# Row maxima of attention as a two-part row: the split moved to columns, the transpose to a product

## The chip, the cores and the metric

The kernel runs on one core of a Trainium2 chip. The core has a matrix engine (TensorE; in the profile PE for its products and PEld for the loading of weights), three elementwise engines (VectorE or DVE, ScalarE or ACT, GpSimd or POOL) and a queue that issues transfers (SyncE or SP). The metric is the device time of one execution in microseconds (us): 1706.35 us for the kernel before, the median of three runs from 1704.84 to 1709.86.

## The reference

One block of a transformer with adaptive layer norm, 2048 tokens of 512 features in fp32:

```python
mod = (_silu(c) @ w_mod).reshape(c.shape[0], 6, 1, -1)
sa, ca, ga, sb, cb, gb = (mod[:, 0], ..., mod[:, 5])
h = _layernorm(x, axis=-1) * (1 + ca) + sa
x = x + ga * attention(h, A_wqkv, A_wo)      # 32 heads of 16, full softmax
h = _layernorm(x, axis=-1) * (1 + cb) + sb
x = x + gb * (mish(h @ B_w1 + B_b1) @ B_w2)  # 512 -> 1792 -> 512
```

The change lies in the softmax of the attention, `softmax(q k^T / 4)`: for each head and each query the maximum over the 2048 keys is taken off before the exponential.

## The kernel before

**Numbers in two parts.** Most products run in float32r, a rounded form of fp32. To keep the precision, a number is split in a high part (rounded to float32r) and a low part (what is left), and a product is made of three: high by high, high by low, low by high. For the attention the split lies along the contraction: a head has 16 features, which become 48 rows of an operand (`ka` for keys, `qa` for queries), two heads to a tile at partitions 0 and 64. Rows 48 to 63 of each half are extra: in `ka` they hold constants (the tile `one`, stored there once in the prologue, copied on for the later buffers), in `qa` zeros, and in rows 48 and 49 of `qa` later the negative maximum of each query in two parts. A score product then gives the score less its maximum at once, since the key's extra rows multiply it by the constants.

**Groups and steps.** Work is cut in 32 groups (`n`): 4 blocks of 512 queries by 8 sets of 4 heads. A group takes 16 steps of the main loop (`step(t)`), each of four kinds of work on TensorE:

- four maxima products (`max_tile`, L482): 128 queries by 512 keys into a slot of a ring of six PSUM banks (`ring()`), each followed by a reduction on VectorE (L484) into a column of `mx`. These belong to a later group: the maxima run 20 steps (`PRO`) ahead of the scores.
- four score products (L531), 128 keys by 512 queries, each into a slot of the same ring, followed by the exponential on ScalarE (L534), which writes `pr`.
- the product of the exponentials with the values (`pv`, L549), called PV below, for the four heads of the step before the last.
- a part of other work (L135): the projections of the first layer, later the output projection and the feed-forward layers, in halves of 64 rows that stand beside the products above.

The order of all instructions is written out by hand: `step` emits maxima and scores in turn, with the other work in between, then PV. Hooks (`at`) put transfers and elementwise work at half steps. A ring slot is taken again six products later, after the reduction or exponential that reads it.

**The rows of maxima.** At the end of the step in which the last maximum of a group is emitted, `neg_max` (L500) reduces the four partial maxima of each query to one. It writes them twice, by two reductions (L505), into `mm`: 128 queries by 32 columns, which are 4 (half and head pair) by 2 (high and low place) by 4 (part of the block). One step later `max_rows` (L509) turns `mm` into rows: a transpose on TensorE against the identity `ident` (L511) into a ring slot, the negated high part rounded to float32r by ScalarE into `mh` (L513), and on VectorE (L514) `mt = mh * lows - slot`, where `lows` is -1 in the rows of the low places and 0 in the others: the high places get the negated maximum rounded by the write, the low ones what is left. Then four transfers of 4 KB (L520) store the rows of `mt` into rows 48 and 49 of the four halves of `qa`. The scores that read them start four steps after the maxima are complete.

Of the kernel before, what the change touches and what calls it, by code (L numbers as in the profile page):

```python
# [8 lines left out]
F32 = mybir.dt.float32  # L9
F32R = mybir.dt.float32r  # L10
AF = mybir.ActivationFunctionType
ALU = mybir.AluOpType
AX = mybir.AxisListType
# [5 lines left out]
def adaln_block(ctx: ExitStack, tc: tile.TileContext, x, wqkv, wo, w1, b1, w2, c, w_mod, out):  # L19
    nc = tc.nc  # L20
    P = 128
# [25 lines left out]
    out = out[0]  # L47
# [3 lines left out]
    cst = ctx.enter_context(tc.tile_pool(name="cst", bufs=1))  # L51
# [11 lines left out]
    ident = cst.tile([P, P], F32, name="ident")  # L63
# [10 lines left out]
    nc.gpsimd.memset(sel, 0.0)  # L74
    for k in range(DK):
        nc.gpsimd.memset(sel[32 * k:32 * k + 1, :], 1.0)
    lows = cst.tile([P, 1], F32, name="lows")
    nc.vector.tensor_reduce(out=lows[:32], in_=ident[:32, :32].rearrange("p (a v q) -> p v a q", a=4, v=2)[:, 1], op=ALU.add,
                            axis=AX.XY)
    nc.vector.tensor_scalar_mul(lows[:32], lows[:32], -1.0)  # L80
    modc = cst.tile([P, 4, DK], F32, name="modc")
    sil = cst.tile([P, DK], F32, name="sil")
    b1c = cst.tile([P, FT], F32, name="b1c")
# [66 lines left out]
    def ring(w=1):  # L150
        if w == 2 and ring_at[0] % 2:
            ring_at[0] += 1
        b = ring_at[0] % NRING
        ring_at[0] += w
        return ring_t[:, b, :] if w == 1 else ring_t[:, b:b + 2, :]
# [41 lines left out]
    def at(h, f):  # L197

        hooks.setdefault(h, []).append(f)
# [121 lines left out]
    with ExitStack() as es:  # L321
# [24 lines left out]
        nc.gpsimd.memset(zer, 0.0)  # L346
        one = lp.tile([P, TB], F32, name="one")
        nc.gpsimd.memset(one, 1.0)

        e = lp.tile([P, DK], F32, name="sil_e")  # L350
        nc.scalar.activation(e, cc, AF.Exp, scale=-1.0)
# [38 lines left out]
        for i in range(2):  # L390
            pr.append(ring())
            for k in range(DK):
                nc.tensor.matmul(pr[i][32 * k:32 * k + 32, :], sil[:, k:k + 1].to_broadcast([P, 32]), wma[i][:, k, :],
                                 start=True, stop=True)
# [68 lines left out]
    ap = ctx.enter_context(tc.tile_pool(name="ap", bufs=1, reuse_waits="tile"))  # L463
# [36 lines left out]
    def neg_max(n):  # L500

        mx = mxs.pop(n)
        mm = ap.tile([P, 4, 2, 4], F32, tag="mm", name="mm", bufs=2)
        for v in range(2):
            nc.vector.tensor_reduce(out=mm[:, :, v, :], in_=mx.rearrange("p s (j q) k -> p (s j) q k", j=2), op=ALU.max,  # L505
                                    axis=AX.X)
        ats.setdefault(16 * n + 16 - PRO, []).append(lambda: max_rows(n, mm))

    def max_rows(n, mm):  # L509
        pt = ring()  # L510
        nc.tensor.transpose(pt[:32, :P], mm.rearrange("p a v q -> p (a v q)"), ident)  # L511
        mh, mt = [ap.tile([32, P], F32R, tag=t, name=t, bufs=1) for t in ("mh", "mt")]
        nc.scalar.activation(mh, pt[:32, :P], AF.Identity, scale=-1.0)  # L513
        nc.vector.scalar_tensor_tensor(mt, mh.bitcast(F32), lows[:32], pt[:32, :P], op0=ALU.mult, op1=ALU.subtract)  # L514

        def put():
            for s in (1, 0):
                for j in range(2):
                    o = (2 * s + j) * 8
                    nc.sync.dma_start(  # L520
                        qa[(2 * n + j) % NR][64 * s + 48:64 * s + 50, :].rearrange("v (s q) -> v s q", s=4).bitcast(F32),
                        mt[o:o + 8, :].bitcast(F32))
        at(2 * (16 * n + 16 - PRO) + 2, put)
# [649 lines left out]
    def step(t):  # L1173
# [4 lines left out]
        if t < 0:  # L1178

            for i in range(2):  # L1180
                if tm < 16:
                    kb, jq = divmod(2 * tm + i, 8)
                else:
                    jq, kb = tm % 16 // 2, 2 * second + i
                max_pair(tm // 16, jq, kb)
            if second and tm % 16 == 15:
                neg_max(tm // 16)
            run_hooks(2 * t + 1)
            for f in ats.pop(t, []):
                f()  # L1190
            whole_units(2 * t + 1, CREDIT)
            do_specials(2 * t + 1)
            return
# [58 lines left out]
        if tm < T and tm % 16 == 15:  # L1252
            neg_max(tm // 16)
# [111 lines left out]
    t = T + 2  # L1365
# [32 lines left out]
```

## Time and profile before

| what | value |
|---|---|
| median of three runs | 1706.35 us (1704.84 to 1709.86) |
| profiled execution, span from first to last instruction | 1705.4 us |
| mean granted TensorE clock | 0.998 of full speed |
| TensorE products busy | 1678.7 us, 98% |
| VectorE busy | 1439.9 us, 84% |
| ScalarE busy | 1364.9 us, 80% |
| GpSimd busy | 808.0 us, 47% |

The span of the profiled execution is 0.95 us below the median of the runs. A row of a timeline gives start and length in us, engine, line, operation, what is written and read, and in brackets the idle time of the engine before it with what ended that time. A group of instructions gives the count after x, busy time in us, the mean of one in ns, and the idle time before them. Products are pipelined and their ends are modelled, so a busy TensorE is not TensorE at its peak.

### The profile page before, as it was taken

What the parts mean: (1) busy time and instruction counts of PE and PEld (TensorE: products, weight loads), DVE (VectorE), ACT (ScalarE), POOL (GpSimd) and SP (SyncE); (2) the same over time, 40 slices, a digit from 0 to 9 for tenths busy, and PEclk for the clock granted to TensorE, in tenths of its full rate; (3) what the DMA queues carried; (4) which work ended last, traced back from release to release, by engine and by line L of the source; (5) the groups of instructions that cost most, each with busy time, mean ns of one, the idle gap of its engine ahead of it and who ended that gap; (6) DMA issues with size and microseconds to landing.
All of it is one profiled execution on the core that took longest, in us unless ns stands there. A gap on an engine that the chain in (4) does not pass through costs nothing.

```text
span 1705.4 us, 33628 instructions
## 1 busy us (share of the span) xinstructions
PE 1678.7 (98%) x12372; PEld 956.8 (56%) x12372; DVE 1439.9 (84%) x2368; ACT 1364.9 (80%) x2613; POOL 808.0 (47%) x829
## 2 busy tenths in 40 slices
PE   7999999999999999999999999999999999999999
PEld 5755655555445555555555555555555455554587
DVE  6888888888889998888889998888889988883377
ACT  6257777777778988888888988888888988888574
POOL 5155224665413464655423564555323655555442
PEclk9999999999999999999999999999999999999999
DMA  7677467777773342534355433424354433524261
GB/s 253 183 235 210 116 161 213 242 228 221 237 209 100 98 105 78 137 79 123 84 154 145 119 75 94 139 74 125 85 144 124 128 93 78 150 59 156 85 228 63
DMA packets 113997, 240.08 MB, mean 141 GB/s; under 512 B 24048, under 2 KB 49648, under 8 KB 107784
## 3 DMA queue, kind: packets, MB, share of 16 engines
q1 hardware_dynamic: 113832, 237.92, 48.8%
q8 instruction: 98, 1.61, 0.4%
q14 instruction: 67, 0.55, 0.1%
HBM read 179.95 MB, written 51.44 MB: 136 GB/s over the span
## 4 chain that ended last, share of the span: by engine, by line
PE 90%; DMA 4%; DVE 3%; ACT 1%; SPq 1%; issue 1%; POOL 0%; ACTq 0%; DVEq 0%; POOLq 0%
PE bk L549 28%; PE ring L482 21%; PE ring L531 19%; PE bk L135 12%; PE bk L129 3%; PE ring L1110 2%; PE ring L129 2%; DVE mx L484 1%; DMA qa<-mt 1%; DMA ka<-kscr 1%; DMA xt<-in_A_x 1%; PE ring L496 1%; ACT pr L534 1%; DMA w<-woscr 1%; DMA w<-w1scr 0%
## 5 line engine op out<-in xcount | busy, mean ns | idle before, releaser
L484 DVE TENSOR_REDUCE mx<-ring 128x1 f32<-128x512 f32 x1968 | 1222.1, 682 | 157.7 <-PE ring L482 134.1
L534 ACT ACTIVATE pr<-ring 128x512 f32<-128x512 f32 x2048 | 1085.6, 601 | 215.5 <-PE bk L135 131.2
L482 PE MATMUL ring<-ka,qa 64*128 64x512 f32 x1968 | 834.2, 427 | 5.2 <-DMA od<-ot 2.7
L531 PE MATMUL ring<-qa,ka 64*128 64x512 f32 x2048 | 724.5, 397 | 4.2 <-ACT pr L534 2.2
L482 PEld LDWEIGHTS ring<-ka,qa 64*128 64x128 f32 x1968 | 359.6, 184 | 405.8 <-DVE mx L484 341.2
L549 PE MATMUL bk<-pr,vg 128*32 128x512 f32 x4096 | 545.1, 604 | 0.0
L531 PEld LDWEIGHTS ring<-qa,ka 64*128 64x128 f32 x2048 | 373.8, 184 | 81.3 <-ACT pr L534 23.6
L135 PE MATMUL bk<-h,w 64*128 64x512 f32 (+1 forms) x1080 | 280.2, 393 | 0.1
L135 PE MATMUL bk<-w,a_h 64*128 64x512 f32 x632 | 213.0, 417 | 0.3 <-ACT pr L534 0.2
L135 PEld LDWEIGHTS bk<-h,w 64*128 64x128 f32 x1080 | 178.2, 184 | 12.3 <-ACT pr L534 3.7
L549 PEld LDWEIGHTS bk<-pr,vg 128*32 128x32 f32 x4096 | 80.7, 108 | 132.0 <-issue 124.6
L135 PE MATMUL bk<-w,a_l 64*128 64x512 f32 x316 | 124.0, 392 | 0.0
L135 PEld LDWEIGHTS bk<-w,a_h 64*128 64x128 f32 x632 | 104.7, 184 | 16.6 <-ACT pr L534 8.3
L899 POOL TENSOR_TENSOR y<-yd,y 128x512 f32<-128x512 f32 x44 | 56.8, 1292 | 89.5 <-ACT yd L898 84.4
L750 POOL TENSOR_TENSOR qq<-qq,rr 128x512 f32<-128x512 f32 x42 | 54.3, 1292 | 89.8 <-ACT rr L744 89.6
L734 POOL TENSOR_SCALAR qq<-ee 128x512 f32<-128x512 f32 x25 | 15.5, 619 | 168.0 <-ACT ee L728 168.0
L736 POOL TENSOR_TENSOR hb<-hb,ee 128x512 f32<-128x512 f32 x42 | 54.1, 1288 | 82.5 <-DVE ee L732 80.5
L135 PE MATMUL bk<-w,o_hl 64*128 64x512 f32 x288 | 79.6, 408 | 0.0
L98 POOL TENSOR_TENSOR a_l<-hb,a_h 128x512 fp32r<-128x512 f32 x53 | 72.0, 1359 | 4.4
L135 PEld LDWEIGHTS bk<-w,a_l 64*128 64x128 f32 x316 | 58.3, 184 | 3.9
L135 PE MATMUL bk<-h_h,wl 64*128 64x512 f32 x168 | 56.7, 418 | 0.0
L752 POOL TENSOR_TENSOR rr<-rr,qq 128x512 f32<-128x512 f32 x42 | 54.2, 1291 | 3.5
(189 smaller groups left out, 1844.2 us busy)
## 6 DMA issues: line engine op xcount, KB each, us to landing
ka<-kscr SPq DMA_DIRECT2D x124, 384.0 KB
w<-w2scr SPq DMA_DIRECT2D x56, 512.0 KB
w<-w1scr SPq DMA_DIRECT2D x46, 512.0 KB
vg<-vscr SPq DMA_DIRECT2D x32, 552.0 KB
qa<-qscr SPq DMA_DIRECT2D x124, 100.0 KB
kscr<-qh SPq DMA_DIRECT2D x16, 512.0 KB
qscr<-qh SPq DMA_DIRECT2D x32, 256.0 KB
hl<-in_B_w SPq DMA_DIRECT2D x28, 256.0 KB
```

The costliest lines, as they stand in the source:

```text
L98: (nc.gpsimd if eng == "p" else nc.vector).tensor_sub(lo, src, hi.bitcast(F32))
L129: nc.tensor.matmul(acc, l, r, start=start, stop=stop)
L135: i = nc.tensor.matmul(acc, l[64 * g:64 * g + 64], r[64 * g:64 * g + 64], start=start and not g, stop=bool(stop and g))
L482: nc.tensor.matmul(pm, qt[64 * s:64 * s + 64, qs * P:(qs + 1) * P], kt[64 * s:64 * s + 64, kb * TB:(kb + 1) * TB], start=True, stop=True)
L484: nc.vector.tensor_reduce(out=mxs[n][:, s, 4 * j + qs, kb:kb + 1], in_=pm, op=ALU.max, axis=AX.X)
L531: nc.tensor.matmul(p_, kt[64 * s:64 * s + 64, kc * P:(kc + 1) * P], qt[64 * s:64 * s + 64, :], start=True, stop=True)
L534: e = nc.scalar.activation(pr, p_, AF.Exp, scale=SCALE)
L549: nc.tensor.matmul(accs[n][32 * h:32 * h + 32, :], vgs[n][:, o:o + 32], pts.pop((t, h)), start=(kc == 0), stop=(kc == 15))
L736: (nc.vector if tail else nc.gpsimd).tensor_mul(hb, hb, ee)
L750: nc.gpsimd.tensor_mul(qq, qq, rr)
L752: nc.gpsimd.tensor_mul(rr, rr, qq)
L899: nc.gpsimd.tensor_add(y[i], yd, y[i])
```

## The change

The split of the maxima moves before the turn into rows. `neg_max` now makes four reductions on VectorE, each with one operand in SBUF: the negative maximum into `nh[:, 0]`; that, negated again and rounded to float32r, into the high places of `mm`; the same into `nh[:, 1]`; and the sum of the two parts of `nh`, the negative of what the rounding left, into the low places of `mm`. The second waits for the first, and the fourth for the third. `mm` becomes float32r, so the turn into rows is an ordinary product with a rounded identity `identr`, and ScalarE copies its result into `mt`. `mh`, `lows` and the VectorE instruction of `max_rows` are gone. The high part now stands with a plus sign, so the first of the key's extra rows is -1: four rows of the tile `one`, which the store spreads as one row of 2048 keys. The order of the products on TensorE, of the instructions on ScalarE and of the transfers is the same as before; on VectorE the four reductions stand where the two stood.

```diff
-    lows = cst.tile([P, 1], F32, name="lows")
-    nc.vector.tensor_reduce(out=lows[:32], in_=ident[:32, :32].rearrange("p (a v q) -> p v a q", a=4, v=2)[:, 1], op=ALU.add,
-                            axis=AX.XY)
-    nc.vector.tensor_scalar_mul(lows[:32], lows[:32], -1.0)
+    identr = cst.tile([P, P], F32R, name="identr")
+    nc.vector.tensor_copy(identr, ident)
...
         one = lp.tile([P, TB], F32, name="one")
         nc.gpsimd.memset(one, 1.0)
+        nc.gpsimd.memset(one[:4, :], -1.0)
...
-        mm = ap.tile([P, 4, 2, 4], F32, tag="mm", name="mm", bufs=2)
-        for v in range(2):
-            nc.vector.tensor_reduce(out=mm[:, :, v, :], in_=mx.rearrange("p s (j q) k -> p (s j) q k", j=2), op=ALU.max,
-                                    axis=AX.X)
+        mm = ap.tile([P, 4, 2, 4], F32R, tag="mm", name="mm", bufs=2)
+        nh = ap.tile([P, 2, 4, 4], F32, tag="nh", name="nh", bufs=1)
+        mx = mx.rearrange("p s (j q) k -> p (s j) q k", j=2)
+        nc.vector.tensor_reduce(out=nh[:, 0], in_=mx, op=ALU.max, axis=AX.X, negate=True)
+        for hi in (mm[:, :, 0, :], nh[:, 1].bitcast(F32R)):
+            nc.vector.tensor_reduce(out=hi, in_=nh[:, 0, :, :, None], op=ALU.max, axis=AX.X, negate=True)
+        with nc.allow_low_precision(reason="the low part of a split"):
+            nc.vector.tensor_reduce(out=mm[:, :, 1, :], in_=nh.rearrange("p v a q -> p a q v"), op=ALU.add, axis=AX.X)
         ats.setdefault(16 * n + 16 - PRO, []).append(lambda: max_rows(n, mm))
 
     def max_rows(n, mm):
         pt = ring()
-        nc.tensor.transpose(pt[:32, :P], mm.rearrange("p a v q -> p (a v q)"), ident)
-        mh, mt = [ap.tile([32, P], F32R, tag=t, name=t, bufs=1) for t in ("mh", "mt")]
-        nc.scalar.activation(mh, pt[:32, :P], AF.Identity, scale=-1.0)
-        nc.vector.scalar_tensor_tensor(mt, mh.bitcast(F32), lows[:32], pt[:32, :P], op0=ALU.mult, op1=ALU.subtract)
+        nc.tensor.matmul(pt[:32, :P], mm.rearrange("p a v q -> p (a v q)"), identr, start=True, stop=True)
+        mt = ap.tile([32, P], F32R, tag="mt", name="mt", bufs=1)
+        nc.scalar.copy(mt, pt[:32, :P])
```

## The prediction

> **What bounds the kernel now.** The page comes first: the busy shares and the chain of work that ended last.
>
> ```profile
> PE 1678.7 (98%) x12372; PEld 956.8 (56%) x12372; DVE 1439.9 (84%) x2368; ACT 1364.9 (80%) x2613; POOL 808.0 (47%) x829
> ...
> PE 90%; DMA 4%; DVE 3%; ACT 1%; SPq 1%; issue 1%; POOL 0%; ACTq 0%; DVEq 0%; POOLq 0%
> ```
>
> TensorE carries 90% of the chain. VectorE is busy 84% of the span but on 3% of the chain, so an edit on it counts only where it makes TensorE wait. Next, the groups by line, each shape apart, for the instructions that the change touches:
>
> ```profile
> L505 DVE TENSOR_REDUCE mm<-mx 128x16 f32<-128x64 f32 x64 | 11.1, 215 | 1.1
> ...
> L514 DVE SCALAR_TENSOR_TENSOR mt<-mh,lows,ring 32x128 fp32r<-32x128 f32 x32 | 10.7, 333 | 15.9 <-ACT mh L513 15.9
> ...
> L511 PE MATMUL ring<-ident,mm 128*32 128x128 f32 x32 | 9.1, 284 | 0.0
> L513 ACT ACTIVATE mh<-ring 32x128 fp32r<-32x128 f32 x32 | 8.5, 266 | 11.0 <-PE ring L511 11.0
> ```
>
> The touched code runs 32 times, once in 16 steps of the main loop; everything on VectorE that goes is 10.7 + 15.9 us busy and idle. How far TensorE sees that is read from the timeline of one boundary between two groups (start, length, engine, instruction, and in brackets idle time and its releaser):
>
> ```profile
> 750.59 0.16 PEld L549 LDWEIGHTS bk<-pr,vg 128*32 128x32 f32 x8 [0.24 <-issue]
> ...
> 751.58 0.18 PEld L482 LDWEIGHTS ring<-ka,qa 64*128 64x128 f32 x1 [0.84 <-DVE mx L484]
> ...
> 751.80 0.35 DVE L505 TENSOR_REDUCE mm<-mx 128x16 f32<-128x64 f32 x2
> ...
> 752.12 2.48 DVE L484 TENSOR_REDUCE mx<-ring 128x1 f32<-128x512 f32 x4
> ...
> 752.86 0.18 PEld L531 LDWEIGHTS ring<-qa,ka 64*128 64x128 f32 x1
> ...
> 753.00 0.18 PEld L482 LDWEIGHTS ring<-ka,qa 64*128 64x128 f32 x1
> ...
> 753.42 0.16 PEld L549 LDWEIGHTS bk<-pr,vg 128*32 128x32 f32 x8 [0.24 <-issue]
> ...
> 754.42 0.09 PEld L511 LDWEIGHTS ring<-ident,mm 128*32 128x32 f32 x1 [0.84 <-DVE mx L484]
> ...
> 754.63 0.18 PEld L482 LDWEIGHTS ring<-ka,qa 64*128 64x128 f32 x1
> ...
> 754.74 0.27 ACT L513 ACTIVATE mh<-ring 32x128 fp32r<-32x128 f32 x1 [0.33 <-PE ring L511]
> ...
> 755.04 0.33 DVE L514 SCALAR_TENSOR_TENSOR mt<-mh,lows,ring 32x128 fp32r<-32x128 f32 x1 [0.44 <-ACT mh L513]
> ...
> 755.31 2.46 DVE L484 TENSOR_REDUCE mx<-ring 128x1 f32<-128x512 f32 x4
> ...
> 755.53 1.52 ACT L534 ACTIVATE pr<-ring 128x512 f32<-128x512 f32 x3
> ...
> 756.03 0.18 PEld L531 LDWEIGHTS ring<-qa,ka 64*128 64x128 f32 x1 [0.17 <-DVE mx L484]
> ...
> 756.15 0.18 PEld L482 LDWEIGHTS ring<-ka,qa 64*128 64x128 f32 x1
> 756.58 0.16 PEld L549 LDWEIGHTS bk<-pr,vg 128*32 128x32 f32 x8 [0.25 <-issue]
> ```
>
> A step runs from one PV block (L549) to the next. The first step is 753.42 - 750.59 = 2.83 us, and TensorE never stops in it: 1.0 us of PV, then from S = 751.58 eight products into the six slots of the ring, the last two loaded at S + 1.28 and S + 1.42, and PV 0.42 after the last load. The two L505 sit in VectorE's pause (751.80 to 752.15), and the step's first reduction starts at S + 0.54, when its product is there: L505 is free now. The second step is 756.58 - 753.42 = 3.16, so 0.33 longer: the transpose holds TensorE 0.21 (754.42 to 754.63), and the rest, 0.12, is the last two loads at S' + 1.40 and S' + 1.52 (S' = 754.63), held by the late reduction (755.31) and by the late exp (755.53 + 0.60).
>
> **What a late first reduction costs** is in two other steps, where other VectorE work went in front:
>
> ```profile
> 1278.47 0.16 PEld L549 LDWEIGHTS bk<-pr,vg 128*32 128x32 f32 x8 [0.37 <-issue]
> ...
> 1279.12 3.05 DVE L484 TENSOR_REDUCE mx<-ring 128x1 f32<-128x512 f32 x5
> ...
> 1279.46 0.18 PEld L482 LDWEIGHTS ring<-ka,qa 64*128 64x128 f32 x1 [0.84 <-DVE ln_mv L105]
> ...
> 1281.02 0.18 PEld L531 LDWEIGHTS ring<-qa,ka 64*128 64x128 f32 x1 [0.33 <-DVE mx L484]
> ...
> 1281.45 0.16 PEld L549 LDWEIGHTS bk<-pr,vg 128*32 128x32 f32 x8 [0.24 <-issue]
> ```
>
> ```profile
> 578.47 0.16 PEld L549 LDWEIGHTS bk<-pr,vg 128*32 128x32 f32 x8 [0.24 <-issue]
> 579.27 3.07 DVE L484 TENSOR_REDUCE mx<-ring 128x1 f32<-128x512 f32 x5
> ...
> 579.46 0.18 PEld L482 LDWEIGHTS ring<-ka,qa 64*128 64x128 f32 x1 [0.84 <-DVE ee L732]
> ...
> 581.20 0.18 PEld L531 LDWEIGHTS ring<-qa,ka 64*128 64x128 f32 x1 [0.41 <-DVE mx L484]
> ...
> 581.63 0.16 PEld L549 LDWEIGHTS bk<-pr,vg 128*32 128x32 f32 x8 [0.24 <-issue]
> ```
>
> In each run of five the first two reductions belong to the step before. At 0.60 apart (0.58 in the first) the third starts at S + 0.82 and S + 1.00 and the load that waits for its slot follows 0.73 later, PV 0.43 after that. The steps are 2.98 and 3.16, 0.15 and 0.33 over 2.83. So a first reduction at S + x costs x - 0.68 us, and nothing below that.
>
> **The change, part by part.** The sum is made against the profiled span of 1705.4; the median of the runs, 1706.35, lies 0.95 above it, and I carry the difference over.
>
> (a) *Four dependent reductions for two, in the step of `neg_max`.* No four-link chain stands in the trace; the nearest rows are L505 and the pair that opens the program:
>
> ```profile
> 1.32 0.16 DVE L78 TENSOR_REDUCE lows<-ident 32x1 f32<-32x16 f32 x1 [1.32 <-POOL ident masks.py:199]
> 1.51 0.14 DVE L80 TENSOR_SCALAR lows<-lows 32x1 f32<-32x1 f32 x1
> ...
> 1313.73 0.18 PEld L482 LDWEIGHTS ring<-ka,qa 64*128 64x128 f32 x1 [0.84 <-DVE mx L484]
> ...
> 1313.89 0.35 DVE L505 TENSOR_REDUCE mm<-mx 128x16 f32<-128x64 f32 x2
> ```
>
> A reduction of 16 elements takes 0.16; a dependent instruction starts 0.03 after the end of its source; independent ones overlap by 0.07 (two L505 of 0.215 in 0.35). First 0.215 + 0.03, second 0.16 but the third starts 0.09 after it, third 0.16 + 0.03, fourth 0.18 (32 elements read), of which the next overlaps 0.07: 0.215 + 0.03 + 0.09 + 0.16 + 0.03 + 0.18 - 0.07 = 0.64 us from start to the step's first reduction. The chain starts at S + 0.16 to S + 0.22 (1313.89 and 751.80), so x is 0.80 to 0.86 instead of 0.54, and the cost 0.12 to 0.18, middle 0.15. Queued behind the two new waits are the step's four big reductions, and behind those TensorE's loads into their slots. VectorE catches up in the next step, where it no longer waits. The regular boundary is there some 27 times of 32: +4.1. Bounds: x 0.07 lower, 0.08 each, +2.2; 0.03 more for each of the three small links, 0.24 each, +6.5.
>
> The Trainium skill has a rule here that speaks against the change: "VectorE: DVE Perf Modes", section "Rules for kernel authors", says to lower the number of operations and not of semaphores, since each operation drains at its full length, chained or not. The trace differs: two independent L505 take 0.35, not 0.43. By the rule (a) would be +5.9 and the sum 1708.9 (rival D has the working).
>
> (b) *L514 and its wait go from VectorE.* The first reduction after the transpose can start at S' + 0.54 instead of S' + 0.68. That frees the load at 756.03, but the one at 756.15 waits for the exp, which the change leaves where it is: `mt` is copied by ScalarE, in the place and at the size of L513 (0.266; I take the copy as equal). Gain between 0 and the whole 0.12; I take 0.04, since the second load stands later: 30 x 0.04 = -1.2. If it is 0, ScalarE is late next. The wait for the former four stores of `mt` moves from L514 to this copy; they were issued 16 steps before and hide there, and queued behind it are this step's exps. Bound +0.03 each, +1.
>
> (c) *An ordinary product in place of the transpose.* Same weights (128x32), 128 moving columns. Nearest rows: L511 itself, 0.21 on TensorE; and the ordinary products into 256 columns, fifteen in 1.99, 0.133 each:
>
> ```profile
> 50.80 1.99 PE bk L129 x15
> ```
>
> Below, half of 0.133 is 0.07: gain 0.14 each, -4.5; above, 0.21 again: 0. I take 0.133, the nearest row of the new kind, as a product of half the columns can hardly be half as dear with its fixed part: 0.08 x 32 = -2.6.
>
> The Trainium skill, "VectorE: DVE Perf Modes", section on the TRN2 errata, gives a product max(60, 6 + columns) cycles at 2.4 GHz: 0.056 us here, an estimate, by which (c) would be -4.9 and the sum 1704.7. No run shows a product of 128 columns; at 256 the trace has 0.133 where the formula gives 0.109.
>
> (d) *Prologue.* In block 0 TensorE waits for the second L505:
>
> ```profile
> 93.47 0.09 PEld L511 LDWEIGHTS ring<-ident,mm 128*32 128x32 f32 x1 [0.36 <-DVE mm L505]
> ```
>
> The chain now ends 0.3 to 0.4 later: +0.4.
>
> (e) *The rest, nothing.* `identr` takes the place of the two `lows` instructions while VectorE waits for the first input. The extra memset of four rows follows L348; the store that reads it is issued 15 us later:
>
> ```profile
> 2.85 0.53 POOL L348 MEMSET one<- 128x512 f32 x1
> ...
> 18.43 0.70 SPq L414 DMA_DIRECT2D ka<-one  x1
> ```
>
> If POOL were busy there it would cost the memset, some 0.3. The 128 stores of `mt` stay, in number, size and order on SP; they now wait for ScalarE instead of VectorE and may start 0.3 earlier, which moves loads behind them forward or not at all. One big reduction per group gets a second wait, for a ScalarE instruction that TensorE has waited past before: nothing.
>
> Sum: 4.1 - 1.2 - 2.6 + 0.4 = +0.7, so 1707.0.
>
> **The rivals.** What can be told from no change is about 0.3%, 5.1 us.
>
> *A: the longer VectorE chain decides (slower).* The place is the step of `neg_max`, the price x - 0.68. For it: that step has no slack beyond 0.14. With (a) at its upper bound and nothing for (b) and (c), a product as dear as the transpose, it is 6.5 + 0.4 = +6.9: 1713.3. It passes +5.1 from x = 0.86. Against it: the 0.03 between dependent instructions.
>
> *B: product and stall both pay in full (faster).* (b) -3.6, (c) -4.5, (a) at its low end +2.2, (d) +0.4: -5.5, 1700.9. For it: TensorE carries the chain. Against: the exp's load stands behind the freed one.
>
> *C: the change doesn't do what it says*: ScalarE's copy waits as VectorE did, and later exps hold the ring: (b) +1, (c) 0, (a) +4.1, (d) +0.4: +5.5, 1711.9. Against it: L513 stood in the same place.
>
> *D: every small reduction takes its full length, no overlap*: 0.215 + 0.16 + 0.16 + 0.18 = 0.715 instead of 0.64, x 0.07 higher, (a) 27 x 0.22 = +5.9, the sum +2.5: 1708.9. Against it: the overlap of the two L505. This is what the Trainium skill's rule in (a) would make of it.
>
> **How the numbers follow.** The forecast has 0.46 and D 0.12, together within 0.3%: 0.58. A and C, slower by over 0.3%: 0.30 (0.22 and 0.08). B, faster by over 0.3%: 0.12. The range takes in C and A, and on the other side all but the end of B: 1702 to 1713.5.
>
> **What would show it.** Right: in the step before each product the load that waits for VectorE shows 0.1 to 0.3 of idle time, PV comes 2.95 to 3.0 after PV; the step with the product shrinks from 3.16 to about 3.05; four small reductions in 0.6 to 0.7. Wrong: if the small reductions take over 0.2 each, if the product holds TensorE over 0.21, or if first reductions at S + 0.8 leave the step at 2.83.

## The result and the profile after

The changed kernel takes 1711.28 us (median of 20 runs, 1708.67 to 1716.11); the kernel before, run between them on the same chip, 1707.68 us (20 runs, 1704.84 to 1712.02). The ratio is 1.002, with an interval of 1.0012 to 1.0028: slower by 3.4 us (2.0 to 4.8), within 0.3%. The forecast was +0.7 us on the 1706.35 of three earlier runs, inside 0.3% too. The sign of the sum was right, its size was not: 2.7 us are missing from it, and the experiments look for them. The two profiled executions lie farther apart than the medians, 1705.4 and 1712.7 us: the changed kernel's was the second longest of its 20 runs, and 2.2 us of the 7.3 lie ahead of the first PV block.

The page of the changed kernel (busy us, share of the span, instructions; then the chain that ended last):

```profile
PE 1686.4 (98%) x12372; PEld 960.9 (56%) x12372; DVE 1441.0 (84%) x2399; ACT 1366.2 (80%) x2613; POOL 810.6 (47%) x830
...
PE 89%; DMA 5%; DVE 3%; ACT 2%; issue 1%; SPq 0%; POOL 0%; ACTq 0%; DVEq 0%; POOLq 0%
```

Shares tell nothing here: VectorE is as busy as before to 1.1 us, and what matters is when. The groups by line of the changed kernel, each shape apart (busy us, mean ns of one | idle time before; the line numbers shift a little from kernel to kernel):

```profile
L516 ACT CAST mt<-ring 32x128 fp32r<-32x128 f32 x32 | 8.2, 255 | 15.0 <-PE ring L514 15.0
L514 PE MATMUL ring<-identr,mm 128*32 128x128 f32 x32 | 7.9, 247 | 0.3 <-DVE mm L509 0.3
L505 DVE TENSOR_REDUCE nh<-mx 128x16 f32<-128x64 f32 x32 | 7.0, 220 | 1.1
L509 DVE TENSOR_REDUCE mm<-nh 128x16 fp32r<-128x32 f32 x32 | 6.0, 187 | 1.1
L507 DVE TENSOR_REDUCE mm<-nh 128x16 fp32r<-128x16 f32 x32 | 5.5, 170 | 1.1
L507 DVE TENSOR_REDUCE nh<-nh 128x16 fp32r<-128x16 f32 x32 | 5.1, 159 | 0.0
```

The timeline shows what they do to the two steps. It is the same boundary between groups as in the prediction (maxima L481/L483, scores L533, exp L536, PV L551):

```profile
755.35 0.16 PEld L551 LDWEIGHTS bk<-pr,vg 128*32 128x32 f32 x8 [0.25 <-issue]
...
756.35 0.18 PEld L481 LDWEIGHTS ring<-ka,qa 64*128 64x128 f32 x1 [0.84 <-DVE mx L483]
...
756.56 0.22 DVE L505 TENSOR_REDUCE nh<-mx 128x16 f32<-128x64 f32 x1
...
756.81 0.17 DVE L507 TENSOR_REDUCE mm<-nh 128x16 fp32r<-128x16 f32 x1
756.90 0.16 DVE L507 TENSOR_REDUCE nh<-nh 128x16 fp32r<-128x16 f32 x1
...
757.09 0.19 DVE L509 TENSOR_REDUCE mm<-nh 128x16 fp32r<-128x32 f32 x1
...
757.20 2.47 DVE L483 TENSOR_REDUCE mx<-ring 128x1 f32<-128x512 f32 x4
...
757.93 0.18 PEld L533 LDWEIGHTS ring<-qa,ka 64*128 64x128 f32 x1 [0.35 <-DVE mx L483]
...
758.00 0.18 PEld L481 LDWEIGHTS ring<-ka,qa 64*128 64x128 f32 x1
...
758.42 0.16 PEld L551 LDWEIGHTS bk<-pr,vg 128*32 128x32 f32 x8 [0.24 <-issue]
...
759.42 0.11 PEld L514 LDWEIGHTS ring<-identr,mm 128*32 128x32 f32 x1 [0.84 <-DVE mx L483]
...
759.60 0.18 PEld L481 LDWEIGHTS ring<-ka,qa 64*128 64x128 f32 x1
...
759.71 0.26 ACT L516 CAST mt<-ring 32x128 fp32r<-32x128 f32 x1 [0.53 <-PE ring L514]
...
760.13 1.89 DVE L483 TENSOR_REDUCE mx<-ring 128x1 f32<-128x512 f32 x3 [0.46 <-PE bk L133]
...
761.12 0.18 PEld L481 LDWEIGHTS ring<-ka,qa 64*128 64x128 f32 x1
...
761.55 0.16 PEld L551 LDWEIGHTS bk<-pr,vg 128*32 128x32 f32 x8 [0.25 <-issue]
```

The step of `neg_max` was 2.83 and is 3.07 (755.35 to 758.42). S is again the first maxima load behind PV, S' the one behind the product. The first big reduction comes at S + 0.85 (757.20 after 756.35), the load that waits for it 0.73 later, with 0.35 of idle time where there was none. The step of the product was 3.16 and is 3.13: the product holds TensorE 0.18 (759.42 to 759.60) where the transpose held it 0.21, and the first big reduction after it comes at S' + 0.53 instead of S' + 0.68, as expected, without the step getting shorter for that. The exps begin at S' + 0.90 as before (755.53 after 754.63, 760.50 after 759.60), and the last load stands at S' + 1.52 as before.

**How the runs are read.** All kernels here have the same 510 PV blocks, so steps can be compared one by one. Over this run, the kernel before and six of the experiments, the steps away from the boundaries differ by 0.016 us in the median and by 0.03 or less in nine of ten. A few steps in blocks 0 and 1 wait for transfers, and these vary from one profiled execution to the next by up to 5.8 us (one of them took 2.86, 3.17, 5.64 and 8.66 in those of four kernels). A timed difference carries that scatter. So the table gives both: the timed difference (ratio less one, by 1708 us) with its interval, and the sum of the differences to the profile of before, step by step, without ten steps that wait for transfers, two of them steps of `neg_max` in block 0.

| kernel | timed, us | steps of `neg_max` | product's step and the next |
|---|---|---|---|
| changed kernel | +3.4 (2.0 to 4.8) | +5.0 | -1.5 |
| chain alone | +4.4 (2.6 to 6.3) | +4.9 | +0.2 |
| L514 gone alone | -2.9 (-4.8 to -1.2) | -0.1 | -0.8 |
| product, short VectorE work | -0.3 (-2.6 to 1.9) | 0.0 | -1.9 |
| chain in two pauses | +4.6 (2.6 to 6.8) | +0.3 | -2.3 |
| one part | -1.9 (-3.9 to 0.2) | -0.3 | -2.4 |
| six links | +16.1 (12.1 to 20.0) | +15.6 | -1.2 |
| five products | +10.4 (7.3 to 13.3) | +4.9 | +5.6 |
| five transposes | +11.4 (8.2 to 14.7) | -0.1 | +13.0 |
| one part, later | -2.9 (-5.5 to -0.2) | +0.1 | -3.4 |
| one part, copy on VectorE | -2.7 (-5.0 to -0.7) | -0.2 | -2.9 |
| two pauses, late groups only | -0.2 (-2.4 to 2.2) | +1.1 | -2.1 |

### The profile page after: what moved, and what is told of

Read it like the earlier page. It is cut to its first block, busy times and chain, and to the rows that moved or that the text cites. A ratio compares the mean times of both kernels' runs of the same rounds, so it can differ in the third digit from the quotient of the medians.

```text
span 1712.7 us, 33682 instructions
## 1 busy us (share of the span) xinstructions
PE 1686.4 (98%) x12372; PEld 960.9 (56%) x12372; DVE 1441.0 (84%) x2399; ACT 1366.2 (80%) x2613; POOL 810.6 (47%) x830
## 4 chain that ended last, share of the span: by engine, by line
PE 89%; DMA 5%; DVE 3%; ACT 2%; issue 1%; SPq 0%; POOL 0%; ACTq 0%; DVEq 0%; POOLq 0%
PE bk L551 28%; PE ring L481 20%; PE ring L533 19%; PE bk L133 12%; PE bk L127 3%; PE ring L1112 2%; PE ring L127 2%; ACT pr L536 1%; DVE mx L483 1%; DMA ka<-kscr 1%; DMA xt<-in_A_x 1%; PE ring L495 1%; DMA qscr<-qh 1%; DMA qa<-mt 1%; DMA woscr<-hl 0%
## 5 line engine op out<-in xcount | busy, mean ns | idle before, releaser
L483 DVE TENSOR_REDUCE mx<-ring 128x1 f32<-128x512 f32 x1968 | 1222.9, 683 | 173.3 <-PE ring L481 134.4
L536 ACT ACTIVATE pr<-ring 128x512 f32<-128x512 f32 x2048 | 1086.3, 601 | 216.1 <-PE bk L133 138.1
L481 PE MATMUL ring<-ka,qa 64*128 64x512 f32 x1968 | 836.9, 429 | 4.1 <-DMA ka<-kscr 2.5
L533 PE MATMUL ring<-qa,ka 64*128 64x512 f32 x2048 | 729.4, 398 | 5.3 <-ACT pr L536 2.1
L481 PEld LDWEIGHTS ring<-ka,qa 64*128 64x128 f32 x1968 | 360.1, 184 | 404.3 <-DVE mx L483 342.4
L551 PE MATMUL bk<-pr,vg 128*32 128x512 f32 x4096 | 545.1, 605 | 0.0
L533 PEld LDWEIGHTS ring<-qa,ka 64*128 64x128 f32 x2048 | 374.4, 184 | 85.4 <-ACT pr L536 23.6
L551 PEld LDWEIGHTS bk<-pr,vg 128*32 128x32 f32 x4096 | 80.8, 108 | 132.2 <-issue 124.9
L133 PEld LDWEIGHTS bk<-w,a_h 64*128 64x128 f32 x632 | 104.7, 184 | 15.6 <-ACT pr L536 8.3
L736 POOL TENSOR_SCALAR qq<-ee 128x512 f32<-128x512 f32 x25 | 15.6, 623 | 167.7 <-ACT ee L730 167.7
```

What stands on the lines that cost most here:

```text
L133: i = nc.tensor.matmul(acc, l[64 * g:64 * g + 64], r[64 * g:64 * g + 64], start=start and not g, stop=bool(stop and g))
L481: nc.tensor.matmul(pm, qt[64 * s:64 * s + 64, qs * P:(qs + 1) * P], kt[64 * s:64 * s + 64, kb * TB:(kb + 1) * TB], start=True, stop=True)
L483: nc.vector.tensor_reduce(out=mxs[n][:, s, 4 * j + qs, kb:kb + 1], in_=pm, op=ALU.max, axis=AX.X)
L533: nc.tensor.matmul(p_, kt[64 * s:64 * s + 64, kc * P:(kc + 1) * P], qt[64 * s:64 * s + 64, :], start=True, stop=True)
L536: e = nc.scalar.activation(pr, p_, AF.Exp, scale=SCALE)
L551: nc.tensor.matmul(accs[n][32 * h:32 * h + 32, :], vgs[n][:, o:o + 32], pts.pop((t, h)), start=(kc == 0), stop=(kc == 15))
```

## The experiments

**The chain alone.** Against the kernel before:

```diff
+        nh = ap.tile([P, 2, 4, 4], F32, tag="nh", name="nh", bufs=1)
+        nc.vector.tensor_reduce(out=nh[:, 0], in_=mx.rearrange("p s (j q) k -> p (s j) q k", j=2), op=ALU.max, axis=AX.X)
         for v in range(2):
-            nc.vector.tensor_reduce(out=mm[:, :, v, :], in_=mx.rearrange(...), op=ALU.max, axis=AX.X)
+            nc.vector.tensor_reduce(out=mm[:, :, v, :], in_=nh[:, 0, :, :, None], op=ALU.max, axis=AX.X)
+        nc.vector.tensor_reduce(out=nh[:, 1], in_=mm.rearrange("p a v q -> p a q v"), op=ALU.add, axis=AX.X)
```

> The kernel before, with only the longer chain on VectorE: four small reductions of the same sizes and dependences as in the changed kernel stand where the two stood (the fourth goes to a place nobody reads); transpose, ScalarE copy and L514 stay. It isolates (a). My theory, from the two profiles: each regular step with the chain is 0.18 to 0.24 us longer, so +3.5 to +5.5 us over the kernel before. The prediction's own price (x - 0.68) gives +4.1 with 0.12 to 0.18 a step. Rival C (the slowdown of the changed kernel lies in the product's step and in ScalarE's copy): +1.5 or less here.

+4.4 us, and +4.9 in the steps that hold the chain, 0.2 in the others of the table. The loss of the changed kernel is the chain; rival C (the product and ScalarE's copy) is out.

**Six links.** Against the changed kernel:

```diff
+        nc.vector.tensor_reduce(out=nh[:, 1], in_=mm[:, :, 1, :].bitcast(F32)[:, :, :, None], op=ALU.max, axis=AX.X)
+        nc.vector.tensor_reduce(out=nh[:, 0], in_=nh[:, 1, :, :, None], op=ALU.max, axis=AX.X)
         ats.setdefault(16 * n + 16 - PRO, []).append(lambda: max_rows(n, mm))
```

> The changed kernel with two more dependent small reductions behind the four (their results are not read). Each link should add 0.16 + 0.03 = 0.19 us, so the first big reduction of the step comes at S + 1.17 instead of S + 0.80. If a late first reduction costs its whole lateness, each regular step becomes 0.37 longer, 27 to 32 times: +10 to +12 us over the changed kernel, +13.5 to +15.5 over the kernel before. If something else in the step absorbs it (the exps, the other work), less than half: +5 or less over the changed kernel.

+16.1 us, 12.7 more than the changed kernel; by the steps of `neg_max` 10.6 more. The timeline of the same boundary with six links:

```profile
757.74 0.16 PEld L553 LDWEIGHTS bk<-pr,vg 128*32 128x32 f32 x8 [0.24 <-issue]
...
758.74 0.18 PEld L481 LDWEIGHTS ring<-ka,qa 64*128 64x128 f32 x1 [0.84 <-DVE mx L483]
...
760.00 1.88 DVE L483 TENSOR_REDUCE mx<-ring 128x1 f32<-128x512 f32 x3
...
760.73 0.18 PEld L535 LDWEIGHTS ring<-qa,ka 64*128 64x128 f32 x1 [0.77 <-DVE mx L483]
...
760.80 0.18 PEld L481 LDWEIGHTS ring<-ka,qa 64*128 64x128 f32 x1
...
761.22 0.16 PEld L553 LDWEIGHTS bk<-pr,vg 128*32 128x32 f32 x8 [0.24 <-issue]
```

The first big reduction is at S + 1.26, the step takes 3.48. Nothing absorbs any of it: with 0.41 more of chain the step is 0.41 longer than in the changed kernel. Both give the same price: the step begins 1.00 ahead of S, the freed load follows the reduction by 0.73, the last load that by 0.07, PV that by 0.42, in all x + 2.22, which is x - 0.61 over 2.83. In the changed kernel x + 2.22 gives the length of 26 of the 30 steps of `neg_max` from the second group to the last but one within 0.01 us. The prediction had x - 0.68. The 0.07 is the last load. In the two steps from which the price came it stood at the instant of the freed one (581.20; 1281.02 and 1281.03); here it comes behind it, and TensorE's queue has an instruction of its own ahead of it. The instructions of the line L481 on TensorE around 758.0, changed kernel (min/median/max ns):

```profile
L481 PEldq EVENT_SEMAPHORE  x1: 51/51/51, 757.9 to 757.9; - x1
```

The kernel before, around 581.2, with no such row:

```profile
L482 PEld LDWEIGHTS ring<-ka,qa x1: 183/183/183, 581.2 to 581.2; 64*128 64x128 f32 x1
```

All 26 steps of `neg_max` in the changed kernel with the 0.07 have such a row for the last load, and in none of its 25 steps whose last two loads come at the same instant is there one. But 15 other steps have 0.06 to 0.07 between their last loads without such a row, so that these 51 ns make the 0.07 is not shown; no run took the instruction away.

**L514 gone, alone.** Against the kernel before (`zl` is a new column of zeros, so the low part of the maxima is left out):

```diff
-        for v in range(2):
-            nc.vector.tensor_reduce(out=mm[:, :, v, :], in_=mx.rearrange(...), op=ALU.max, axis=AX.X)
+        for v, src in enumerate((mx.rearrange(...), zl.to_broadcast([P, 64]).rearrange(...))):
+            nc.vector.tensor_reduce(out=mm[:, :, v, :], in_=src, op=ALU.max, axis=AX.X)
...
-        nc.scalar.activation(mh, pt[:32, :P], AF.Identity, scale=-1.0)
-        nc.vector.scalar_tensor_tensor(mt, mh.bitcast(F32), lows[:32], pt[:32, :P], op0=ALU.mult, op1=ALU.subtract)
+        nc.scalar.activation(mt, pt[:32, :P], AF.Identity, scale=-1.0)
```

> The kernel before, with only L514 gone from VectorE: still two independent small reductions (the second reads zeros, so the low part of each maximum is left out and only the high part is stored; both score sides are shifted alike), still the transpose; ScalarE writes the rows directly. It isolates (b). The prediction: -1.2 us (-0.04 in each step with the transpose). My theory after seeing both profiles: the exp on ScalarE holds the step, so 0 to -0.7 us, although the first big reduction there starts 0.13 earlier. Rival B: -3.6 us, 0.12 in each such step.

The steps with the transpose, its timeline:

```profile
754.36 0.16 PEld L550 LDWEIGHTS bk<-pr,vg 128*32 128x32 f32 x8 [0.25 <-issue]
755.36 0.09 PEld L513 LDWEIGHTS ring<-ident,mm 128*32 128x32 f32 x1 [0.84 <-DVE mx L486]
...
756.11 1.89 DVE L486 TENSOR_REDUCE mx<-ring 128x1 f32<-128x512 f32 x3 [0.58 <-PE bk L137]
...
757.09 0.18 PEld L484 LDWEIGHTS ring<-ka,qa 64*128 64x128 f32 x1
757.52 0.16 PEld L550 LDWEIGHTS bk<-pr,vg 128*32 128x32 f32 x8 [0.25 <-issue]
```

The reduction comes 0.75 after the load of the transpose instead of 0.89 (754.42 and 755.31 before), and the step is 3.16 as before; in the median of all such steps the difference is 0.00. The -0.8 in the table is four irregular steps. So (b) is worth nothing in these steps. The timed -2.9 us says more than the steps do, and its interval leaves out -0.8; no part of the trace that repeats from run to run holds the rest. It may lie in the steps that wait for transfers, whose scatter is as large; this stays open.

**Product with short VectorE work.** The changed kernel with two independent reductions for the four:

```diff
-        nc.vector.tensor_reduce(out=nh[:, 0], ...)
-        ... (the other three)
+        for v, src in enumerate((mx.rearrange("p s (j q) k -> p (s j) q k", j=2), zl.to_broadcast(...)...)):
+            nc.vector.tensor_reduce(out=mm[:, :, v, :], in_=src, op=ALU.max, axis=AX.X)
```

> The changed kernel with two independent small reductions in place of the chain of four (the second reads zeros, so the low part of the maxima is left out), the product and the ScalarE copy kept. It isolates (b) + (c). The prediction: -1.2 - 2.6 = -3.8 us against the kernel before. My theory from the profiles: the step with the product is 0.03 to 0.05 shorter than the one with the transpose, so -1 to -1.6 us, with the product holding TensorE 0.17 to 0.18. Rival B: -8 us. Rival C: 0 or slower.

-0.3 us (-2.6 to 1.9), and -1.9 by the steps. The regular steps with the product come in two kinds: 12 of 3.16 before, where on ScalarE an instruction of the feed-forward stands between the copy of the rows and the exps, and 14 of 3.11, where none does. They are now 3.12 and 3.07, 0.04 less in each. That is (c) whole, since (b) is nothing: half of what the prediction gave it. Rival B is out.

**The price of one product and of one transpose.** `for _ in range(5):` ahead of the product of the changed kernel, and ahead of the transpose of the kernel before.

> The changed kernel with the product of 128 columns made five times in a row into the same slot. 4 x 32 more products: at 0.133 each (the prediction) +17 us over the changed kernel; at 0.18 +23; at 0.056 (the Trainium skill's formula, an estimate) +7. The timeline of five in a row shows the price of one on TensorE directly.

> The kernel before with the transpose made five times in a row into the same slot. 4 x 32 more transposes: at 0.21 each (what the prediction read from 754.42 to 754.63) +27 us over the kernel before. If the difference between the two operations in a row is 0.08 each, as the prediction has it, this run stands 10 us farther from its base than the run with five products; if it is 0.03, 4 us.

Five products, then five transposes, the load of the first and the next load of another kind:

```profile
761.59 0.32 PEld L515 LDWEIGHTS ring<-identr,mm 128*32 128x32 f32 x5 [0.84 <-DVE mx L483]
...
762.01 0.18 PEld L481 LDWEIGHTS ring<-ka,qa 64*128 64x128 f32 x1
```

```profile
758.78 0.44 PEld L512 LDWEIGHTS ring<-ident,mm 128*32 128x32 f32 x5 [0.84 <-DVE mx L484]
...
759.43 0.18 PEld L482 LDWEIGHTS ring<-ka,qa 64*128 64x128 f32 x1 [0.21 <-issue]
```

Five products hold TensorE 0.42 where one held it 0.18: 0.06 for each further one. Five transposes hold it 0.65 where one held it 0.21: 0.11 each. The timed +7.0 over the changed kernel is 0.055 for each of the 128 added products; the +11.4 of the transposes is 0.09 for each, and the steps' 13.0 is 0.10. Alone, in 31 of the 32 places, a transpose holds TensorE 0.214 to 0.216 and a product 0.175 to 0.179. So one product is 0.06 with about 0.12 around it, one transpose 0.11 with about 0.10 around it, and the exchange gains the difference of the sums, 0.04, not that of the marginal prices. The Trainium skill's formula ("VectorE: DVE Perf Modes", the section on the TRN2 errata), 0.056 by its figures, an estimate, agrees with a product behind another of its kind, 0.055 to 0.06; the 0.18 of a single one between other work it does not give.

**The chain in two pauses.** The changed kernel with the third and fourth reduction one step later, and product, copy and stores one step later with them:

```diff
-        for hi in (mm[:, :, 0, :], nh[:, 1].bitcast(F32R)):
-            nc.vector.tensor_reduce(out=hi, ...)
-        ... (the fourth)
-        ats.setdefault(16 * n + 16 - PRO, []).append(lambda: max_rows(n, mm))
+        nc.vector.tensor_reduce(out=mm[:, :, 0, :], ...)
+        ats.setdefault(16 * n + 16 - PRO, []).append(lambda: neg_low(n, mm, nh))
+    def neg_low(n, mm, nh):
+        ... (the third and the fourth)
+        ats.setdefault(16 * n + 17 - PRO, []).append(lambda: max_rows(n, mm))
...
-        at(2 * (16 * n + 16 - PRO) + 2, put)
+        at(2 * (16 * n + 17 - PRO) + 2, put)
```

> The changed kernel with the same four small reductions, two of them in VectorE's pause where they stand now and two in the pause one step later; product, copy and stores of the rows come one step later (two steps before the scores that read them, instead of three). If the price of (a) is the late first reduction alone, each pause holds its half, (a) goes to about 0 and the time is that of (b) + (c): 1 to 1.6 us below the kernel before, 4.5 to 6 below the changed one. Rival: the rows arrive too late for the scores, or the stores collide with other transfers one step later: no better than the changed kernel, +3 us or more, with TensorE waiting for the stores of the rows.

> The chain of four in two pauses again, but only from the tenth group on; the groups before keep the chain, the product and the stores where the changed kernel has them. If the run with two pauses lost its gain to rows that came late in groups 5 to 8 and in the prologue, this one waits for the rows no longer than the kernel before, pays (a) nine times at 0.15 to 0.24 (+1.5), and has the later steps at or below those of the kernel before (-1.5 to -2.2): within 1 us of the kernel before, about 3 below the changed one. Rival (the two halves cost what the chain cost): no better than the changed kernel, +3 us or more.

The first of them is as slow as the changed kernel, +4.6, although its steps are 2.0 below those of before. The waits of TensorE (line waited for: us in total, times, longest) point to why; the kernel with two pauses, then the kernel before:

```profile
PEld ring L537 <- DMA qa<-mt: 6.5, 3, 2.5
...
PE ring L537 <- DMA qa<-mt: 5.8, 4, 2.2
```

```profile
PEld ring L531 <- DMA qa<-mt: 1.6, 2, 0.9
PE ring L531 <- DMA qa<-mt: 1.2, 3, 0.6
```

The rows arrive late for the scores of three early groups, in steps of 4.58, 5.09 and 5.76 that were 2.85, 3.50 and 3.77. These are among the steps that vary by themselves, and so are the waits: in the traces of the kernels that keep these groups' early place they are 0.4 to 4.8 us. One trace can't carry the reading, so the second kernel is the test. With the early place kept for the first nine groups (`16 + (n > 8)` in place of 17, and `neg_low` at once for the others) the kernel is back at -0.2 us, and waits 0.8 and 0.4 us for the rows in place of 6.5 and 5.8. From the tenth group on the late halves cost nothing (0.02 or less beside the same steps with one part), save in three groups, where VectorE came into the second pause with a big reduction left over and the step is some 0.3 longer. In two irregular steps of `neg_max` the first two reductions still cost 0.21. So the price of (a) is one of place: the same four reductions cost 0.2 in one pause of VectorE and mostly nothing in two.

**One part.** The changed kernel with the maximum rounded and taken off as it is, in one row:

```diff
-        mm = ap.tile([P, 4, 2, 4], F32R, tag="mm", name="mm", bufs=2)
-        ... (nh and the four reductions)
+        mm = ap.tile([P, 4, 4], F32R, tag="mm", name="mm", bufs=2)
+        nc.vector.tensor_reduce(out=mm, in_=mx.rearrange("p s (j q) k -> p (s j) q k", j=2), op=ALU.max, axis=AX.X)
...
-                        qa[(2 * n + j) % NR][64 * s + 48:64 * s + 50, :]...
+                        qa[(2 * n + j) % NR][64 * s + 48:64 * s + 49, :]...
```

> The changed kernel with one small reduction instead of four: the maximum, rounded to float32r, is taken off as it is, in one part (the low part is left out; softmax takes any shift that numerator and denominator share). 16 columns in the product instead of 32, stores of 2 KB instead of 4 KB. Theory: nothing is late on VectorE, (b) and (c) remain, and the prologue waits 0.15 less: -1 to -2.5 us against the kernel before. Rival B: -8 us.

-1.9 us (-3.9 to 0.2), -2.7 by the steps: what is left of the change without its price. Two variants of it follow, the first with `16 + (n > 8)` for 16 in the two places above, the second with `nc.vector.tensor_copy(mt, ...)` for `nc.scalar.copy(mt, ...)`.

> The changed kernel with one small reduction and one part (the low part is left out), and from the tenth group on the product, the copy and the stores one step later. In the run with the chain in two pauses the product's step cost 0.18 where it stands one step later (3.02 against 2.84) and 0.22 to 0.27 where it stands in the changed kernel; the scores waited for late rows only in groups 5 to 8, which here keep the early place. Theory: the 0.04 to 0.09 less 22 times, -1 to -2 us beside the run with one part, -3 to -4 us against the kernel before. Rival: the rows come late in some of the later groups too: 0 or slower against the kernel before.

> The run with one part (the low part is left out), with the copy of the rows out of the ring slot made by VectorE instead of ScalarE. It asks what holds the step with the product, where taking L514 from VectorE gained nothing. If ScalarE's late exps hold it, that step gets shorter than the 3.06 of the run with one part wherever VectorE has a pause in it (about 3.01 to 3.03), and longer where VectorE comes out of the step before with a reduction left over (the copy in front of the first big reduction, 3.10 before, 3.15 to 3.2 here); over all within 1 us of the run with one part. If TensorE itself holds it (the product and the extra slot), 3.06 stays in the former and the latter do not get shorter either.

The later place gives -2.9 us (-5.5 to -0.2), the copy on VectorE -2.7 (-5.0 to -0.7); both are below the kernel before by a little more than the scatter, and which of the three is best these runs cannot tell. Nor can the timed runs tell them from the kernel before with L514 gone (-2.9), which keeps the transpose and leaves out the low part too; by the steps that one gained less (-0.9). The copy on VectorE answers why (b) was worth nothing, and not as expected. In the kind of step with 3.06 (3.11 before) it changes nothing. In the kind with 3.10 (12 steps, 3.16 before) the step falls to 2.99 to 3.06, though VectorE got the work (in five of them the next step gives 0.05 to 0.07 back). One of these steps, one part with the copy on ScalarE, then on VectorE:

```profile
754.53 0.18 PEld L481 LDWEIGHTS ring<-ka,qa 64*128 64x128 f32 x1
754.64 0.26 ACT L510 CAST mt<-ring 16x128 fp32r<-16x128 f32 x1 [0.28 <-PE ring L508]
...
754.80 0.72 ACT L737 ACTIVATE rr<-ee,two 128x512 f32<-128x512 f32 x1
...
755.42 1.52 ACT L530 ACTIVATE pr<-ring 128x512 f32<-128x512 f32 x3
...
756.05 0.18 PEld L481 LDWEIGHTS ring<-ka,qa 64*128 64x128 f32 x1
```

```profile
758.11 0.72 ACT L737 ACTIVATE rr<-ee,two 128x512 f32<-128x512 f32 x1
...
758.38 0.18 PEld L481 LDWEIGHTS ring<-ka,qa 64*128 64x128 f32 x1
...
759.15 1.62 ACT L530 ACTIVATE pr<-ring 128x512 f32<-128x512 f32 x3 [0.33 <-PE ring L527]
...
759.80 0.18 PEld L481 LDWEIGHTS ring<-ka,qa 64*128 64x128 f32 x1
```

On ScalarE the copy pushes an instruction of the feed-forward (L737) and with it the exps: they begin 0.89 after the first maxima load, and the last load stands at 1.52. Without the copy they begin at 0.77 and the last load stands at 1.42, where it stands in a step with no product at all. So there ScalarE holds the step, and taking work from VectorE gains nothing. In the other kind, with no such instruction in front, the product's own time is the whole price. From the tenth group on, the run with one part, later, has these steps without a product, and there they take 2.89 to 2.90; one of them:

```profile
847.34 0.16 PEld L545 LDWEIGHTS bk<-pr,vg 128*32 128x32 f32 x8 [0.24 <-issue]
...
850.23 0.16 PEld L545 LDWEIGHTS bk<-pr,vg 128*32 128x32 f32 x8 [0.24 <-issue]
```

With the 0.16 for which the product of 16 columns holds TensorE that is 3.05 to 3.06, with the 0.18 of 32 columns 3.07, with the 0.21 of the transpose 3.11: the lengths measured with one part, in the changed kernel and before. The first kind takes 2.83 to 2.87 without a product, so there the same sum leaves 0.10 over, and that is what the copy on ScalarE costs.

## Why the prediction was right, and where not

The forecast of a time within 0.3%, and its main mechanism, were right: a late first reduction in the step of `neg_max` is paid by TensorE, the rest is small. With 20 runs of each kernel the slowdown can be told from none all the same. Step by step:

- **(a) +4.1 forecast, +5.0 by the steps, +4.4 timed with the chain alone.** The chain came out at the working's 0.64 us (756.56 to 757.20), with x at 0.80 and 0.85; dependent reductions follow 0.03 apart, the independent third starts 0.09 after the second. As the prediction read the Trainium skill's rule ("VectorE: DVE Perf Modes", "Rules for kernel authors"), it would have been the sum of the four lengths measured here, 0.74; the trace has 0.64, which rules out rival D's chain. The term that was mis-sized is the price, x - 0.68: it is x - 0.61, because in the steps it was read from the last load came together with the freed one. What a regular step paid was 0.16 to 0.26 instead of 0.12 to 0.18. That the sum is not farther off is luck in the count: "27 regular boundaries" was too many. 18 steps were 2.83 to 2.87 before and paid 3.8 together; in six that were already 2.93 to 3.00 the chain cost 0.02 to 0.14, 0.4 together; two irregular ones paid 0.4 each. With the measured price, 27 would have given +5.7.
- **(b) -1.2 forecast, 0 in the steps.** The reduction came earlier by 0.14 to 0.15, as worked out. The taken 0.04 was a guess between 0 and 0.12; the lower end was the case. In 12 steps the reason is "ScalarE is late next", as the copy on VectorE shows; in the other kind there was nothing to gain, since the transpose's own time makes the whole step. The timed -2.9 of L514 gone stays without an explanation.
- **(c) -2.6 forecast, about -1.4** (31 times 0.04 is -1.2, the table has -1.5). The step that failed is the choice of 0.133 from products of 256 columns in a run of fifteen. That row has the price of a product behind its like, and the 0.21 it was taken from was a whole, with its fixed part. Of the two in a row, 0.06 and 0.11, or of the two alone, 0.177 and 0.215, either pair gives 0.04 to 0.05.
- **(d) +0.4 forecast.** From the start of the small reductions to the load of the product it was 93.03 to 93.47 before; after, 95.14 to 95.91. That is 0.33 more; before, then after:

```profile
93.03 0.34 DVE L505 TENSOR_REDUCE mm<-mx 128x16 f32<-128x64 f32 x2
```

```profile
95.14 0.22 DVE L505 TENSOR_REDUCE nh<-mx 128x16 f32<-128x64 f32 x1
...
95.91 0.11 PEld L514 LDWEIGHTS ring<-identr,mm 128*32 128x32 f32 x1 [0.71 <-DVE mm L509]
```

- **(e)** is not told apart from the scatter of the prologue's loads: the first PV block comes 2.2 us later than before in the changed kernel's trace, and 0.3 to 2.8 later in those of the experiments, the ones without the chain among them. The extra memset took 0.52 where the prediction set some 0.3; the store that reads it is issued 16 us later (19.71 after 3.46).

With the measured terms the sum is 5.0 + 0 - 1.4 + 0.3 = +3.9, against +3.4 timed. Each of the three misses pushed the same way. Of all the sums, rival D's +2.5 came nearest, but its chain of full lengths is not what the trace has, so that is luck; A (+6.9) and C (+5.5) were too slow. Of the signs named ahead, the four small reductions took 0.64, inside 0.6 to 0.7; the wait of the load was 0.26 to 0.38 in most regular steps instead of 0.1 to 0.3, the step 3.02 to 3.09 instead of 2.95 to 3.0, the product's step 3.07 and 3.12 instead of 3.05.

## What to carry to other kernels

A price read from a neighbouring step holds only if that step ends the same way: compare the last instructions ahead of its end too, not only the stall. An operation that replaces another is priced whole against whole or margin against margin; a margin from a run of fifteen against a single whole invents a gain. And where timed runs scatter by some us, steps laid beside each other one by one resolve some 0.03 us here, which is what an edit of this size needs; the same step with the operation moved away tells how much of it is the operation's own.

## What was not expected of the hardware

- A transpose of a 128x32 fp32 tile costs 0.11 us behind another, a float32r product of the same shape 0.06; a single one between other work has 0.10 to 0.12 more, whichever it is (0.21 and 0.18).
- A wait can be an instruction of its own in TensorE's queue (51 ns). In the 26 places of the changed kernel where one belongs to the last load of a step of `neg_max`, that load comes 0.07 behind the freed one; without one the two come at the same instant in some steps and up to 0.13 apart in others.
- The same step took from 2.86 to 8.66 us in the traces of different kernels where it waits for a transfer, while nine of ten steps without such a wait repeat within 0.03.
